# The first stage and the weight folds put into the written list, and a table that names each tile's buffer

## The chip, the cores and the metric

The kernel runs on one core of one Trainium2 chip, whose granted TensorE clock is 0.997 of full speed in the profiled execution. The metric is the device time of one execution in microseconds (us). The time before is the median of three runs, 713.57 us (712.26 to 713.77).

## The reference

A residual network of four blocks, A, B, A, B, over 2048 tokens of width 576, all in float32, each block on the layer norm of its input:

```python
x = x + A(layernorm(x))   # linear attention: 32 heads of 18; q, k, v = x @ wqkv; phi = elu + 1
x = x + B(layernorm(x))   # 32 heads; per head the best of 8 keys k1 and the best of 8 keys k2
                          # pick one of 64 experts; out = sum gelu(x . u[e]) * v[e]
x = x + A(layernorm(x))   # same weights again
x = x + B(layernorm(x))
```

In B the scores are `(x @ w_q) . k`. Since `w_q` (576 x 32 x 256) meets only the 8 keys of each half, the kernel first folds the keys into the weights: 64 products of 128 x 576 by the keys, one for each head and half. The result is a table of 576 x 448 that serves both B blocks.

## The kernel before, in words

The tokens lie in 16 tiles of 128 rows. The four blocks form two layers (l = 0 and 1), each with a front (`fT` transposes the normalised tile into a high and a low part, `k`, `v` and `q` multiply it by the projections, `st` adds phi(k) times v to the running state `kva`) and a back (`num`, `oT`, `O` for the attention output, `bT`, `S` for the transposed tile and its scores, `sel` and `gel` for the choice of experts, `po` for the output). A product of a tile with a 576-wide weight is 28 matmuls: 14 passes over high and low parts, two column ranges each (lines 269 and 504). Products are named `ppk_t`, `ppv_t`, `ppq_t`, `ppo_t` and `pps_t` after what they make and the tile.

Some transposes do not go through TensorE (the table SQUARES names them, from tile 4 on in the first front): VectorE turns 32 x 32 squares (`rf`, line 239), one DMA writes the tile to DRAM (`y_df`), and four DMAs read it back transposed (`gf`, line 248); ScalarE and VectorE then split it into `thi` and `tlo` (lines 124 and 126).

**The folds.** Group m of the 64 loads `wq_t[:, m, :]` (288 KB, 128 x 576) by one DMA (`fold_load`, line 654) and multiplies it by a 128 x 32 piece of the padded keys `kpad` (`fold_mm`, line 664). The 32 result rows of group m land in partitions `32*j` to `32*j + 32` of one PSUM tile, with j = m mod 4:

```python
        a, j = divmod(i, 4)                      # i = m % 16
            nc.tensor.matmul(p[32 * j:32 * j + 32, at:at + c1 - c0], kpad[:, ch // 2, 24 - 8 * a:56 - 8 * a],
                             st[:, c0:c1], start=(a == 0), stop=(a == 3))
```

So a fold matmul uses 32 of the array's 128 columns: column tile j. Each group has two matmuls, one of 320 columns and one of 256. Sixteen groups fill one PSUM tile; `fold_out` (line 668 on) then copies it out, transposes it and splits it into `shi` and `slo`, the score weights.

**What sets the order.** Each engine executes its instructions in the order in which the program holds them. Up to tile 10 of layer 0 a Python loop writes them: per tile t = 2 to 9 it emits the loads of eight fold groups, the products k, v and q of the tile, and then the eight fold groups m = 8(t-2) to 8(t-2)+7 in ascending order (`for m in groups: fold_mm(m)`). From there on the order is written out as a long list of pieces, `play("...")`: the word `k0.10` runs the next piece of front_k of layer 0 and tile 10, up to the point at which the piece hands back control. The pieces of PE, ScalarE, VectorE and GpSimd are tied to the order of the program in both parts (`in_order`); the DMA-issuing queue SP is tied in the list alone, and the order of the transfers of the loop is left to the framework. All transfers are issued by SP, each of which waits for the one eight before it.

**Buffers.** Each kind of tile has a ring of a few buffers (`x1` 6, `pq` 2, `x2` 2, `s` 2, `thi` and `tlo` 4 and so on), and a new tile takes the next one of its ring. The fold loads go through `x1`, `pq`, `x2` and `s`, in a fixed sequence of ten.

Of the kernel before, what the change touches and what calls it, by code (L numbers as in the profile page):

```python
# [11 lines left out]
F32 = mybir.dt.float32  # L12
# [9 lines left out]
S, D, H, DH = 2048, 576, 32, 18  # L22
# [40 lines left out]

@with_exitstack
def network(ctx, tc, x_in, wqkv, wo, wq_t, k_t, u_t, v2, c_mask, c_mask4, c_ident, c_code, c_code1, c_scale, c_shift, out):
# [5 lines left out]
    dr = ctx.enter_context(tc.tile_pool(name="dr", bufs=1, space=DRAM))  # L71

# [60 lines left out]
    BUFS = {"pq": 2, "s": 2, "x1": 6, "x2": 2}  # L133
# [514 lines left out]

    fold_ps = {}
    fold_st = {}  # L650

    def fold_load(m):
        st = fold_st[m] = stage(f"fold{m}")
        nc.sync.dma_start(st, wq_t[:, m, :])

    def fold_mm(m):
        st = fold_st.pop(m)
        ch, i = divmod(m, 16)
        if i == 0:
            fold_ps[ch] = psum(f"fold_ps{ch}")  # L660
        p = fold_ps[ch]
        a, j = divmod(i, 4)
        for c0, c1, at in ((0, 320, 0), (320, D, 512)):
            nc.tensor.matmul(p[32 * j:32 * j + 32, at:at + c1 - c0], kpad[:, ch // 2, 24 - 8 * a:56 - 8 * a],  # L664
                             st[:, c0:c1], start=(a == 0), stop=(a == 3))
# [46 lines left out]
    def small_loads():  # L712
# [16 lines left out]

    vu = {}  # L730

    def load_vu(l, t):
        sv = stage("vst")
# [3 lines left out]
        su = stage("ust")[:, :NB * NE].rearrange("p (b e) -> p b e", b=NB)  # L737
# [28 lines left out]
    def ok(t):  # L766
        return 0 <= t < NT
# [27 lines left out]
    def pair(t):  # L795
        return ((st, t - 1), (st, t)) if t % 2 else ()

    def play(text, at=0):

        for w in text.split():  # L800
# [5 lines left out]
                  fo=fold_out, bc=bc, bT=exp_y, cT=exp_c, S=S, sel=sel, gel=gel, po=po, keep=keep, rl=rl, lq=lq, ldx=ldx, ldq=ldq, base=base)  # L806
# [10 lines left out]
    with in_order(*ALL):  # L817
# [36 lines left out]
        small_loads()  # L854
        split_weight(wq_in, 0, whi, wlo, REM, (0,))
# [7 lines left out]
        PER, FIRST = 8, 10  # L863
        for t in range(2, FIRST):
            m0 = PER * (t - 2)
            groups = range(m0, m0 + PER)
            done = (m0 - 1) // 16 if m0 % 16 == 0 and m0 else None
            if t == 2:
                first_load(0, 4)
                run(0, (ln, 3))  # L870
            else:
                run(0, (fT, t + 1, 1))
            for m in groups[:4]:
                fold_load(m)
# [12 lines left out]
            run(0, (v, t), (q, t), (fT, t + 1), *pair(t))
            for m in groups:
                fold_mm(m)
    with in_order(*ALL, ET.SP):  # L890

        play("""
            lv0.0 fl0.13 fo0.3 fT0.11x2 wl1.0 ln0.12 fl0.14 fT0.11 fl0.15 ln0.12x2 ln0.13x2 lv0.0 ld0.1 v0.10 k0.10
            fT0.12x2 v0.10x2 ln0.13 k0.10x2 fo0.3 fT0.13 fT0.11 q0.10x2 fT0.11 v0.11 ln0.15 k0.11 v0.11 ld0.1 v0.11
            q0.10 q0.11 ln0.15 sv0.0 fT0.12 ln0.14x3 fT0.12 fT0.13 k0.11 ld0.0 fT0.12 k0.12 v0.12 k0.12 k0.11 st0.11
            st0.10 q0.12 k0.12 fT0.13x2 v0.12x2 ln0.15 fT0.13 fT0.15 k0.13 wl0.0 q0.12x2 k0.13x2 wl0.0 q0.10 fT0.15x3
            v0.13 fT0.15 k0.15 fT0.14 v0.15 v0.13x2 st0.12 st0.13 q0.11x2 fT0.14x3 v0.15x2 fT0.14 k0.14x2 v0.14 q0.13
            v0.14x2 k0.14 k0.15x2 st0.14 st0.15 wl0.0 ld0.2 ld0.0 wl0.0 mk0.0x2 q0.13x2 zs0.0x2 wl0.0 q0.11 num0.0x3
            M0.1x2 M0.2x2 num0.1 M0.3x2 q0.14x2 num0.0x2 oT0.0 M0.0 M0.4 num0.1 ld0.2 ld0.3x2 num0.1x3 oT0.1 oT0.0x2
            M0.0 num0.2 M0.4 oT0.0 oT0.1 O0.0 num0.2x4 O0.0x2 q0.14 oT0.2x2 O0.0x3 oT0.1x2 O0.1x3 bT0.0 num0.3 oT0.2x2  # L900
            O0.2 num0.3x3 bT0.0x2 O0.1x2 q0.12 num0.3 S0.0x2 ld0.4x2 O0.2 O0.1 bT0.1 num0.4 S0.0 num0.4x2 O0.2 bT0.1
            gel0.0x2 ld0.6 gel0.0 sel0.0 q0.15 sel0.0x2 ld0.5 q0.15 gel0.0 bT0.1 q0.15 O0.2x2 sel0.0 oT0.3x3 S0.1x3
            num0.4 cT0.0x3 num0.4 oT0.3 O0.3 O0.2 gel0.1 sel0.1x2 gel0.1x3 O0.3 bT0.2x2 po0.0x4 ld0.6 po0.0 bT0.2
            O0.3x2 sel0.1x2 oT0.4x3 S0.2x2 O0.3 S0.2 gel0.2 O0.3 oT0.4 cT0.1x2 O0.4 sel0.2 po0.0x2 fT1.0x2 cT0.1 ld0.5
            po0.1 O0.4 num0.5 po0.1 fT1.0 bT0.3x3 po0.1x2 gel0.2x2 O0.4 po0.1 O0.4 ld0.7x2 O0.4x2 q0.13 v1.0 sel0.2
            keep1.0 k1.0 v1.0x2 sel0.2 num0.5 gel0.2 sel0.2 po0.1 q0.14 po0.1 cT0.2 num0.5 cT0.2x2 fT1.1x2 k1.0
            keep1.0 S0.3x2 po0.2 num0.6 num0.5 num0.6 S0.3 gel0.3 bT0.4x2 num0.6 fT1.1 keep1.1 num0.5 keep1.1 num0.6
            po0.2x2 sel0.3 k1.0 oT0.5x2 k1.1 oT0.5x2 v1.1 num0.6 oT0.6x2 num0.7 bT0.4 po0.2 gel0.3 po0.2 sel0.3x2 S0.4
            gel0.3 S0.4 num0.7x3 gel0.3 sel0.3 v1.1 k1.1x2 v1.1 po0.2 S0.4 cT0.3x2 po0.2 gel0.4 sel0.4x2 num0.7
            gel0.4x2 cT0.3 oT0.6 ld0.8x2 oT0.6 O0.5x2 fT1.2x2 po0.3x2 fT1.2 O0.5 keep1.2 O0.5x3 bT0.5 st1.0 st1.1  # L910
            oT0.6 bT0.5 v1.2 po0.3 oT0.7 po0.3 oT0.7 bT0.5 po0.3x3 fT1.3x3 oT0.6 v1.2 num0.8x2 ld0.10 v1.2 O0.6 gel0.4
            O0.6x3 bT0.5 sel0.4x2 k1.2 bT0.5 k1.2 num0.8x2 k1.2 cT0.4x3 S0.5 fT1.3 S0.5 fT1.3 po0.4x2 O0.6x2 bT0.6
            S0.5 oT0.7 po0.4x3 gel0.5 sel0.5 bT0.6 num0.8 oT0.8x2 po0.4 oT0.7 po0.4 bT0.6 oT0.7 fT1.4x2 sel0.5 oT0.7
            v1.3 ld0.10 gel0.5x2 ld0.9 v1.3 fT1.4 v1.3 sel0.5 O0.7x2 k1.3 gel0.5 sel0.5 cT0.5 bT0.6 cT0.5 O0.7x2 st1.2
            k1.3 bT0.6 O0.7x2 cT0.5 po0.5x2 ld0.9 k1.3 fT1.4 keep1.3 bT0.7 num0.10 S0.6x3 num0.10 keep1.3 gel0.6x2
            fT1.4 v1.4 gel0.6 sel0.6x3 bT0.7 po0.5x4 oT0.8 po0.5 fT1.5 num0.10 oT0.8 num0.9x2 v1.4 gel0.6 oT0.8
            num0.10 num0.9 k1.4x2 bT0.7x2 keep1.2 num0.9x2 oT0.9 fT1.5 oT0.8 O0.8x2 bT0.7 S0.7x2 k1.4 O0.8 sel0.6
            cT0.6 O0.8 fT1.5 st1.3 fT1.5 oT0.9 cT0.6 ld0.11x2 cT0.6 po0.6 fT1.5 keep1.5 k1.5 po0.6 O0.8 oT0.9 S0.7
            gel0.7 sel0.7 O0.8 po0.6x3 bT0.8x2 sel0.7 po0.6x2 fT1.6x2 bT0.8 keep1.5 oT0.9x2 v1.5 v1.4 gel0.7 num0.10
            oT0.10x2 k1.5 sel0.7 gel0.7 k1.5 fT1.6 keep1.4 oT0.9 ld0.12 gel0.7 O0.9 sel0.7 cT0.7 st1.4 bT0.8 num0.11x2  # L920
            bT0.8 O0.9 cT0.7 O0.9x2 S0.8x2 v1.5 fT1.6 cT0.7 po0.7 fT1.6 oT0.10 keep1.6 O0.9x2 po0.7 num0.11 bT0.9
            po0.7 k1.6 po0.7x2 v1.5 po0.7 num0.11 S0.8 sel0.8 po0.7 fT1.7 oT0.10 gel0.8 bT0.9 gel0.8x2 oT0.10 num0.11
            sel0.8 ld0.12 oT0.10 fT1.7 sel0.8 k1.6 oT0.11 v1.6 bT0.9 gel0.8 sel0.8 v1.6x2 fT1.7 num0.12 k1.6 O0.10x2
            oT0.11 bT0.9x2 O0.10 keep1.4 num0.12 ld0.13 cT0.8x3 num0.12x3 O0.10x2 oT0.12 S0.9 st1.5 S0.9 fT1.7x2 po0.8
            S0.9 gel0.9 oT0.11 q0.15 po0.8 oT0.12 O0.10 bT0.10 po0.8 gel0.9 oT0.11 gel0.9 bT0.10 po0.8x3 v1.7x3
            oT0.11x2 O0.11 ld0.13 po0.8 k1.7 bT0.10x2 gel0.9 sel0.9x2 num0.13 fT1.8x3 sel0.9x2 cT0.9 st1.6 oT0.12
            O0.11x4 num0.13x2 bT0.10 num0.13 S0.10x2 num0.13 cT0.9x2 po0.9 fT1.8x2 v1.8 po0.9x3 O0.11 S0.10 gel0.10
            bT0.11x2 ld0.14x2 po0.9x2 sel0.10x2 k1.7x2 gel0.10x2 po0.9 bT0.11 oT0.13 fT1.9x2 sel0.10 k1.8 oT0.12x2
            oT0.13 bT0.11 keep1.7 bT0.11 fT1.9 oT0.12 O0.12 S0.11 k1.8 O0.12 num0.14 S0.11 gel0.10 keep1.6 sel0.10
            O0.12 v1.8x2 cT0.10 num0.14 O0.12 k1.8 ld0.15 cT0.10x2 st1.7 po0.10 oT0.13 po0.10x2 fT1.9x2 v1.9 S0.11  # L930
# [92 lines left out]
```

## Time and profile before

| What | us |
|---|---|
| median of 3 runs | 713.57 |
| the profiled execution | 712.88 |
| span of its instructions | 711.1 |
| TensorE matmuls busy | 695.5 |
| TensorE weight loads busy | 649.1 |
| VectorE busy | 466.2 |
| ScalarE busy | 321.3 |
| GpSimd busy | 202.2 |

The engines are named PE (matmuls), PEld (weight loads, which overlap matmuls), DVE (VectorE), ACT (ScalarE), POOL (GpSimd) and SP (the queue that issues DMAs). L269 is line 269 of the kernel. Matmul ends are modelled, so a record lasts longer than the matmul holds the array. In a view by time stretches, each row gives an engine's busy time in the stretch and, after the x, how many of its instructions overlap the stretch. A row of waits gives the total, the number and the longest wait in us. A row in order of time gives start, length, what ran, its shape, its count and, in brackets, the idle time before it and what ended it.

### The profile page before, as it was taken

What the parts mean: (1) busy time and instruction counts of PE and PEld (TensorE: products, weight loads), DVE (VectorE), ACT (ScalarE), POOL (GpSimd) and SP (SyncE); (2) the same over time, 40 slices, a digit from 0 to 9 for tenths busy, and PEclk for the clock granted to TensorE, in tenths of its full rate; (3) what the DMA queues carried; (4) which work ended last, traced back from release to release, by engine and by line L of the source; (5) the groups of instructions that cost most, each with busy time, mean ns of one, the idle gap of its engine ahead of it and who ended that gap; (6) DMA issues with size and microseconds to landing.
All of it is one profiled execution on the core that took longest, in us unless ns stands there. A gap on an engine that the chain in (4) does not pass through costs nothing.

```text
span 711.1 us, 14610 instructions
## 1 busy us (share of the span) xinstructions
PE 695.5 (98%) x5464; PEld 649.1 (91%) x5464; DVE 466.2 (66%) x1005; ACT 321.3 (45%) x658; POOL 202.2 (28%) x544
## 2 busy tenths in 40 slices
PE   8999999999999999999999899999999999999996
PEld 5999989998998999999999899999999999999984
DVE  5543343445327787788888687651556798888896
ACT  4522332242314455556555555543544534454443
POOL 2210100011003444434344343210144343444331
PEclk9999999999999999999999999999999999999998
DMA  9947878754230325467775666342631144311111
GB/s 268 297 136 244 278 227 258 248 158 131 93 116 18 101 72 188 126 190 221 241 232 164 213 211 185 112 142 83 205 123 53 55 124 127 103 65 51 50 69 50
DMA packets 82712, 107.17 MB, mean 151 GB/s; under 512 B 8977, under 2 KB 47377, under 8 KB 82641
## 3 DMA queue, kind: packets, MB, share of 16 engines
q1 hardware_dynamic: 82640, 106.24, 47.2%
q8 instruction: 43, 0.70, 0.4%
q14 instruction: 29, 0.23, 0.1%
HBM read 68.88 MB, written 37.32 MB: 149 GB/s over the span
## 4 chain that ended last, share of the span: by engine, by line
PE 81%; DVE 7%; DMA 4%; issue 2%; ACT 2%; SPq 1%; POOL 1%; DVEq 0%; ACTq 0%; POOLq 0%
PE ppo L504 15%; PE ppq L269 15%; PE ppk L269 13%; PE ppv L269 13%; PE pps L546 8%; PE kva L546 4%; PE kva L376 3%; PE fold_ps L664 2%; PE po L631 2%; PE ptb L225 2%; DMA y_df<-rf 2%; PE pto L225 1%; PE m L431 1%; PE ppq L281 1%; DMA xf<-in_x 1%
## 5 line engine op out<-in xcount | busy, mean ns | idle before, releaser
L504 PE MATMUL ppo<-ohi,thio 126*128 126x252 f32 (+1 forms) x320 | 50.5, 300 | 0.1
L269 PE MATMUL ppk<-whi,thif 128*128 128x252 f32 (+1 forms) x300 | 45.5, 298 | 1.4 <-ACT thif L124 1.4
L504 PEld LDWEIGHTS ppo<-ohi,thio 126*128 126x128 f32 (+1 forms) x320 | 44.8, 189 | 0.8 <-issue 0.3
L269 PEld LDWEIGHTS ppk<-whi,thif 128*128 128x128 f32 x300 | 40.9, 188 | 4.6 <-issue 2.9
L269 PE MATMUL ppv<-whi,thif 128*128 128x252 f32 (+1 forms) x300 | 44.6, 295 | 0.2 <-ACT thif L124 0.2
L269 PE MATMUL ppv<-whi,tlof 128*128 128x252 f32 (+1 forms) x300 | 44.0, 293 | 0.1
L187 POOL TENSOR_SCALAR rsf<-mvf 128x1 f32<-128x1 f32 x16 | 3.4, 213 | 142.9 <-DVE mvf L184 142.8
L269 PE MATMUL ppk<-whi,tlof 128*128 128x252 f32 (+1 forms) x300 | 43.9, 293 | 0.0
L197 ACT ACTIVATE junk<-x,mb 128x576 bf16<-128x576 f32 x32 | 24.8, 774 | 40.6 <-POOL mb L195 40.4
L269 PEld LDWEIGHTS ppv<-whi,thif 128*128 128x128 f32 x300 | 41.3, 188 | 1.4 <-ACT thif L124 0.8
L269 PEld LDWEIGHTS ppv<-whi,tlof 128*128 128x128 f32 x300 | 41.2, 188 | 0.3 <-DVE tlof L126 0.3
L269 PEld LDWEIGHTS ppk<-whi,tlof 128*128 128x128 f32 x300 | 41.2, 188 | 0.0
L471 POOL TENSOR_TENSOR o<-pq,zb 128x576 f32<-128x576 f32 x19 | 27.4, 1442 | 47.1 <-ACT zb L416 45.7
L215 ACT ACTIVATE yb<-x,rsb 128x640 f32<-128x640 f32 x32 | 29.4, 918 | 24.5 <-POOL rsb L204 24.4
L504 PE MATMUL ppo<-olo,thio 126*128 126x252 f32 (+1 forms) x256 | 39.6, 293 | 0.0
L504 PE MATMUL ppo<-ohi,tloo 126*128 126x252 f32 (+1 forms) x256 | 39.5, 293 | 0.0
L269 PE MATMUL ppq<-whi 128*128 128x252 f32 (+1 forms) x260 | 39.4, 298 | 0.0
L289 DVE TENSOR_SCALAR ek<-ek 128x576 f32<-128x576 f32 x16 | 7.3, 459 | 48.5 <-ACT ek L287 48.5
L269 PEld LDWEIGHTS ppq<-whi 128*128 128x128 f32 x260 | 36.1, 188 | 0.3
L504 PEld LDWEIGHTS ppo<-olo,thio 126*128 126x128 f32 x256 | 36.2, 189 | 0.0
L269 PE MATMUL ppk<-wlo,thif 128*128 128x252 f32 x240 | 36.1, 293 | 0.0
L269 PE MATMUL ppv<-wlo,thif 128*128 128x252 f32 x240 | 36.1, 293 | 0.0
(211 smaller groups left out, 1770.8 us busy)
## 6 DMA issues: line engine op xcount, KB each, us to landing
fold<-in_wq_t SPq DMA_DIRECT2D x64, 288.0 KB, 4.2
whi<-hl_d SPq DMA_DIRECT2D x26, 320.0 KB, 4.0
y_df<-rf SPq DMA_DIRECT2D x23, 320.0 KB, 2.3
gf<-y_df SPq DMA_DIRECT2D x92, 80.0 KB, 2.4
pq_d<-eq SPq DMA_DIRECT2D x19, 288.0 KB, 5.4
pq<-pq_d SPq DMA_DIRECT2D x19, 288.0 KB, 5.7
xf<-in_x SPq DMA_DIRECT2D x16, 288.0 KB, 4.5
x<-in_x SPq DMA_DIRECT2D x16, 288.0 KB, 3.5
```

What stands on the lines that cost most here:

```text
L197: nc.scalar.activation(junk, xt, AF.Square, bias=m[:, 0:1], accum_out=m[:, 1:2])
L215: nc.scalar.activation(y, x2, AF.Identity, scale=rs[:, 0:1], bias=rs[:, 1:2])
L225: nc.tensor.transpose(pt[:, b * P:(b + 1) * P], x, ident)
L269: nc.tensor.matmul(o[:, at:at + c1 - c0], tt[a == "lo"][:, b, :], wb[:, cols + c0:cols + c1], start=(i == 0), stop=(i == len(todo) - 1))
L281: nc.tensor.matmul(p[:, at:at + c1 - c0], tt[a == "lo"][:, b, :], wb[:, cols + c0:cols + c1], start=(i == 0), stop=(i == len(todo) - 1))
L289: nc.vector.tensor_scalar(e, e, 1.0, EPS, op0=ALU.min, op1=ALU.add)
L376: nc.tensor.matmul(a[64 * h:64 * h + 64, c * 72:c * 72 + n], vt[:, 2 * c + h], fk[:, f0:f0 + n], start=(t == 0 and c == 0), stop=(t == NT ...
L471: nc.gpsimd.tensor_tensor(o[:, :D], pq, zb, op=ALU.mult)
L504: nc.tensor.matmul(p[:, at:at + c1 - c0], hl[a][:r, b], w[:r, c0:c1], start=(i == 0), stop=(i == len(todo) - 1))
L546: nc.tensor.matmul(p[:, :512], hl[a == "lo"][:, b, :], shi[:, b] if w == "hi" else slo[:, blocks(REM)[b][1]], start=(i == 0), stop=(i == l ...
L631: nc.tensor.matmul(p[:, at:at + c1 - c0], c[i], vmix[:, c0:c1], start=(i == 0 and not based), stop=(i == 1))
L664: nc.tensor.matmul(p[32 * j:32 * j + 32, at:at + c1 - c0], kpad[:, ch // 2, 24 - 8 * a:56 - 8 * a], st[:, c0:c1], start=(a == 0), stop=(a ...
```

## The change

Three things are done together.

1. The loop over tiles 2 to 9 is gone. The pieces of these tiles stand in the written list, which is tied for SP too, and the whole list, layer 1 included, is a new one. Fold loads and fold matmuls are pieces of it (`ml0.13`, `mm0.13` for group 13). The first ten fold loads stand ahead of the list, with the loads of x tiles 4 and 5, and the four mask loads move between them.
2. The fold loads go through a sequence of 14 buffers, which takes in the two buffers of kind `o`.
3. A table SLOTS has for each kind of tile a string of digits; the n-th tile of the kind takes the buffer that the n-th digit names.

The work of each engine is the same: as many instructions of each kind on PE, DVE, ACT, POOL and SP.

```diff
+SLOTS = {
+    "x": "012012102102102012010210120102102100212010101021",
+    "x1": "012345012345021352314250312354315402145052314052310523102310214350214350124",
...
+    "thi": "0123012301320130012012031203123120101210210201212031203123012301230230230231021302",
+    "tlo": "0123012301320130012012031203213212020021010010020003330030201212010101010120310231",
...
+class Slots:
+    def __init__(self, pool, bufs):
+        self.pool, self.bufs, self.at = pool, bufs, {k: iter(v) for k, v in SLOTS.items()}
+
+    def tile(self, shape, dtype, tag, name, bufs=None):
+        bufs = bufs or self.bufs
+        if tag in self.at:
+            tag, bufs = f"{tag}_{next(self.at[tag])}", 1
+        return self.pool.tile(shape, dtype, tag=tag, name=name, bufs=bufs)
...
+    FOLD = ["x1", "pq", "x2", "s", "x1", "o", "x1", "pq", "x2", "s", "x1", "x1", "o", "x1"]
...
-    def fold_load(m):
-        st = fold_st[m] = stage(f"fold{m}")
+    def fold_load(l, m):
+        tag = FOLD[m % len(FOLD)]
+        st = wk.tile([P, D + 56 * (tag == "o")], F32, tag=tag, name=f"fold{m}", bufs=BUFS[tag])[:, :D]
+        fold_st[m] = st
         nc.sync.dma_start(st, wq_t[:, m, :])
 
-    def fold_mm(m):
+    def fold_mm(l, m):
...
-    with in_order(*ALL):
+    with in_order(*ALL, ET.SP):
...
         small_loads()
+        run(0, (fl, 4), *((fold_load, m) for m in range(6)), (fl, 5))
+        mask_loads()
+        run(0, *((fold_load, m) for m in range(6, 10)))
...
-        PER, FIRST = 8, 10
-        for t in range(2, FIRST):
-            m0 = PER * (t - 2)
-            groups = range(m0, m0 + PER)
...
-            run(0, (v, t), (q, t), (fT, t + 1), *pair(t))
-            for m in groups:
-                fold_mm(m)
-    with in_order(*ALL, ET.SP):
 
         play("""
-            lv0.0 fl0.13 fo0.3 fT0.11x2 wl1.0 ln0.12 fl0.14 fT0.11 fl0.15 ln0.12x2 ln0.13x2 lv0.0 ld0.1 v0.10 k0.10
...
+            ml0.13 ln0.4x3 ml0.18 k0.2 fl0.7 k0.2 ln0.3 fl0.9 fT0.4 ml0.11 ln0.3 k0.2 ln0.3 ml0.26 ln0.5x3 fT0.5 fT0.4
+            v0.2x2 fT0.3 q0.2 fT0.5 ln0.7x2 mm0.0 mm0.2 mm0.1 v0.2 fT0.3 mm0.6 mm0.5 fl0.6 mm0.3 fT0.3 q0.2x2 ln0.9
+            mm0.4 ln0.6 ln0.7 mm0.8 ln0.9 mm0.9 fT0.7 ml0.27 mm0.13 ml0.16 mm0.7 ml0.10 mm0.11 v0.3x3 fl0.10 k0.3 q0.3
...
```

**The folds on PE.** Before, the first eight fold groups stand on PE behind the products of tile 2. In the rows, `fold1_562` is the load of group 1, and 32x320 is a result of 32 rows and 320 columns.

```order
L664 MATMUL fold_ps0_698<-fold0_560,kpad_76 32x320
L664 MATMUL fold_ps0_698<-fold0_560,kpad_76 32x256
L664 MATMUL fold_ps0_698<-fold1_562,kpad_76 32x320
L664 MATMUL fold_ps0_698<-fold1_562,kpad_76 32x256
L664 MATMUL fold_ps0_698<-fold2_564,kpad_76 32x320
L664 MATMUL fold_ps0_698<-fold2_564,kpad_76 32x256
L664 MATMUL fold_ps0_698<-fold3_566,kpad_76 32x320
L664 MATMUL fold_ps0_698<-fold3_566,kpad_76 32x256
```

All eight runs of the loop are of this kind: the groups go through column tiles 0, 1, 2, 3 and again 0, 1, 2, 3. In the changed program PE has nine runs of 12, 4, 8, 8, 6, 10, 7, 6 and 3 groups. This is the third, behind the product k of tile 4:

```order
L712 MATMUL fold_ps1_1059<-fold16_784,kpad_76 32x320
L712 MATMUL fold_ps1_1059<-fold16_784,kpad_76 32x256
L712 MATMUL fold_ps1_1059<-fold20_952,kpad_76 32x320
L712 MATMUL fold_ps1_1059<-fold20_952,kpad_76 32x256
L712 MATMUL fold_ps1_1059<-fold18_584,kpad_76 32x320
L712 MATMUL fold_ps1_1059<-fold18_584,kpad_76 32x256
L712 MATMUL fold_ps1_1059<-fold22_963,kpad_76 32x320
L712 MATMUL fold_ps1_1059<-fold22_963,kpad_76 32x256
L712 MATMUL fold_ps1_1059<-fold26_638,kpad_76 32x320
L712 MATMUL fold_ps1_1059<-fold26_638,kpad_76 32x256
```

It goes on with groups 17, 21 and 25. Its groups follow one another by column tile: 0, 0, 2, 2, 2, 1, 1, 1. The nine runs hold these groups, in this order: (0 2 1 6 5 3 4 8 9 13 7 11), (15 10 12 14), (16 20 18 22 26 17 21 25), (19 23 29 24 27 31 30 28), (32 34 33 35 39 43), (36 47 37 41 40 44 45 38 42 46), (48 52 56 51 49 53 57), (50 54 58 62 55 60), (61 59 63).

**The turned tile 12 on SP.** Before, the write of tile 12's turned squares stands behind the loads of u (`ust`, line 740 on) for the experts:

```order
L700 DMA xf_15_1985<-in_x 128x576
L740 DMA ust_2002<-in_u_t 128x64 x2
L742 DMA ust_2002<-in_u_t 64x64
L743 DMA ust_2002<-in_u_t 64x64
L740 DMA ust_2002<-in_u_t 128x64 x2
L453 DMA x0_1_2009<-in_x 128x576
L242 DMA y_df0_12_2071<-rf0_12_2069 128x640
```

Now it stands among the fold loads, 44 rows ahead of the loads of u:

```order
L702 DMA fold51_1688<-in_wq_t 128x576
L702 DMA fold57_1690<-in_wq_t 128x576
L293 DMA gf0_9_1693<-y_df0_9_1110 32x4x160 x4
L287 DMA y_df0_12_1753<-rf0_12_1585 128x640
L748 DMA xf_13_1755<-in_x 128x576
L702 DMA fold48_1791<-in_wq_t 128x576
```

**The kept low part of tile 6 on SP.** For layer 1 some transposed tiles are written to DRAM (`front_keep`, `hl_d`), and the buffers of `thi` and `tlo` come free when the write has landed. Before, that of the low part of tile 6 stands behind the reads `gf1_9`, which wait for the write `y_df1_9`:

```order
L248 DMA gb0_11_5307<-y_db0_11_5272 32x4x160 x4
L242 DMA y_df1_9_5316<-rf1_9_5314 128x640
L242 DMA y_do0_13_5357<-ro0_13_5312 128x640
L347 DMA hl_d7_97<-thif1_7_4982 128x640
L248 DMA gf1_9_5364<-y_df1_9_5316 32x4x160 x4
L349 DMA hl_d6_96<-tlof1_6_4726 128x640
```

Now it stands 16 rows ahead of tile 11's own write `y_db0_11`:

```order
L293 DMA gb0_9_4853<-y_db0_9_4788 32x4x160 x4
L287 DMA y_df1_7_4909<-rf1_7_4858 128x640
L392 DMA hl_d6_96<-thif1_6_4731 128x640
L394 DMA hl_d6_96<-tlof1_6_4732 128x640
L293 DMA gf1_7_4927<-y_df1_7_4909 32x4x160 x4
```

More of the change, by code (lines that the diff above doesn't have):

```diff
@@ L728, in small_loads, with mask_loads @@
         nc.gpsimd.memset(digit, 63)
+    def mask_loads():
+        nc.sync.dma_start(mask[:63, :72], c_mask[:63, 7:79])
+        nc.sync.dma_start(mask[64:127, :72], c_mask[63:, 61:])
+        for r in (0, 64):
+            nc.sync.dma_start(mask[r:r + 36, 72:], c_mask[:36, 7:43])
     vu = {}
     def load_vu(l, t):
-        sv = stage("vst")
+        sv = stage("vst", 9)
         nc.sync.dma_start(sv[:64], v2)
@@ L736, in load_vu @@
         yield 1
[L737 removed]
+        su = stage("ust", 10)[:, :NB * NE].rearrange("p (b e) -> p b e", b=NB)
         for b, (r, bl) in enumerate(blocks(REM)):
```

243 lines of the change are left out of this document (129 added, 114 removed).

## The prediction

> **What bounds the kernel now.** I read the page first, then TensorE by stretches, then who it waits for.
>
> ```profile
> span 711.1 us, 14610 instructions
> PE 695.5 (98%) x5464; PEld 649.1 (91%) x5464; DVE 466.2 (66%) x1005; ACT 321.3 (45%) x658; POOL 202.2 (28%) x544
> ...
> 0.00:40.00 40.00, 36.28 (x273) 31.33 (x274) 22.92 (x39) 18.00 (x32) 9.97 (x28) 1.00 0.84 266
> 40.00:150.00 110.00, 110.00 (x1083) 100.31 (x1082) 44.36 (x89) 34.62 (x84) 8.04 (x24) 1.00 0.72 229
> 150.00:232.00 82.00, 79.67 (x671) 76.56 (x670) 39.81 (x80) 27.79 (x59) 10.36 (x23) 1.00 0.34 100
> 232.00:460.00 228.00, 226.07 (x1705) 213.41 (x1704) 178.72 (x392) 126.52 (x265) 93.97 (x247) 1.00 0.55 174
> 460.00:660.00 200.00, 199.69 (x1483) 189.94 (x1482) 139.82 (x304) 93.24 (x181) 64.71 (x174) 1.00 0.33 102
> 660.00:711.10 51.10, 43.80 (x260) 37.51 (x258) 40.59 (x105) 21.16 (x44) 15.14 (x49) 0.96 0.16 59
> ...
> PE kva L546 <- DVE tlob L126: 1.9, 1, 1.9
> ```
>
> PE is the bound: 15.6 of 711.1 us idle. The start (3.7 idle) is the same code in both programs, and its first products stand in the same order; the end (7.3 idle) is the last tiles' chain, which the new list leaves nearly as it was. Between 40 and 660 us only 4.6 us of idle time are to be had, and three waits are most of it: the 1.9 of the last row, and 1.35 and 0.63 that are quoted below. The stretch that the change rewrites, 40 to 150, has none: 110.00 of 110.00 us busy, at full clock, with the DMA engines at 0.72. So a new order can gain little there, and whatever makes PE's own work longer there is paid in full.
>
> **The change part by part.**
>
> *The folds.* Fold groups are the one work whose length on PE depends on the order. These rows are the second run of eight groups (which ends where the next product starts), then the first run, cut into short stretches:
>
> ```profile
> 62.01 2.19 PE L664 MATMUL fold_ps<-fold,kpad 128*32 128x320 f32 x32
> 64.12 0.38 PE L269 MATMUL ppk<-whi,thif 128*128 128x252 f32 x1
> ...
> L664 PE MATMUL fold_ps<-fold,kpad x256: 378/406/458, 47.4 to 149.0; 128*32 128x320 f32 x64, 128*32 128x256 f32 x64
> ...
> 47.40:47.46 0.06, 0.05 (x4) 0.05 (x6) 0.00 (x0) 1.00 0.50 115
> 47.46:47.70 0.24, 0.24 (x4) 0.13 (x8) 0.00 (x0) 1.00 0.88 326
> 47.70:47.76 0.06, 0.06 (x8) 0.05 (x4) 0.00 (x0) 1.00 0.77 307
> 48.19:48.24 0.05, 0.05 (x8) 0.04 (x1) 0.00 (x0) 1.00 0.14 46
> 48.24:48.40 0.16, 0.16 (x8) 0.07 (x1) 0.00 (x0) 1.00 0.12 43
> 48.40:48.46 0.06, 0.06 (x8) 0.05 (x6) 0.00 (x0) 1.00 0.00 0
> 49.16:49.23 0.07, 0.07 (x9) 0.00 (x0) 0.00 (x0) 1.00 0.00 0
> ```
>
> A run of eight takes 64.12 - 62.01 = 2.11 us. A group leaves 256 / 64 = 4 matmul records. In the cut rows four records begin at once (x4 at 47.40), nothing begins until 47.70, then four more (x8: four ending, four beginning), and so on; 48.19 begins the fourth round, 48.40 the first of the second four groups. So the four column tiles run side by side, and within its tile a group holds 48.40 - 47.40 = 1.00 us for its four records, one after the other; the second four begin their last record at 49.16 and are through after one more record of 0.21 to 0.22 (the distance from 48.19 to 48.40), 0.98 us after their start. I call 0.98 us a slot. A run of two slots takes 2.11 = 2 x 0.98 + 0.15 of change-over. Two groups in one tile never overlap.
>
> The row 48.24:48.40 tells how far PE looks ahead. All four tiles began their last record by 48.24, yet until 48.40 only one weight load runs, that of group 4; the other groups' loads begin at 48.40 together with the first matmul of group 4. So a group is not let in until the one before it in the program has begun. From that I take the rule of my forecast: groups begin in program order, each as soon as its tile is free and its predecessor has begun.
>
> Is a group quicker when it has the array alone? The state fold is float32 over the whole array with nothing beside it:
>
> ```profile
> 216.84 3.15 PE L431 MATMUL m<-wob,kvb 127*126 127x288 f32 x12
> 219.61 1.17 PE L269 MATMUL ppq<-whi,thif 128*128 128x252 f32 x6
> ```
>
> (219.61 - 216.84) / 12 = 0.23 us per record of 288 columns, 0.80 ns per column. A fold record takes 1.00 / 4 = 0.25 for 288 columns on the mean (320 and 256), 0.87 ns per column, with three others beside it. So the rate looks like that of a float32 record anywhere, and a lone group should still take its slot.
>
> Now the new runs. In (16 20 18 22 26 17 21 25) the tiles are 0 0 2 2 2 1 1 1. By the rule they begin in slots 0, 1, 1, 2, 3, 3, 4, 5 and the run ends after 6: 6 x 0.98 + 0.15 = 6.0 us where the loop's order took 2.11. Counted alike, the nine runs take 5, 2, 6, 4, 3, 5, 5, 4 and 2 slots, together 36: 36 x 0.98 + 9 x 0.15 = 36.6 us. Before, 8 x 2.11 = 16.9. Term: **+19.7 us**, with no idle time in the stretch to take it.
>
> The Trainium skill, "TensorE: Matmul & The Clock Gate", Part 3 on packing small matmuls, says that matmuls start and end strictly in program order. By that rule group 0's four records would end before group 1's first, a group would cost 0.98 us in any order, 64 x 0.98 = 62.7 us before and after, and the order would change nothing. This case's trace disagrees: four groups begin within 0.06 us.
>
> *State updates.* PE has 22 runs of state matmuls instead of 20, two pairs being cut in half.
>
> ```profile
> 293.84 1.43 PE L376 MATMUL kva<-ek,v 128*64 128x72 f32 x40
> 321.34 0.81 PE L376 MATMUL kva<-ek,v 128*64 128x72 f32 x20
> ```
>
> 2 x 0.81 - 1.43 = 0.19 each: **+0.4**.
>
> *The three waits.*
>
> ```profile
> 152.78 0.84 DVE L239 STREAM_TRANSPOSE rf<-yf 128x640 f32<-128x640 f32 x1 [1.34 <-ACT yf L215]
> 154.75 0.85 SPq L740 DMA_DIRECT2D ust<-in_u_t  x2
> 158.44 0.38 SPq L242 DMA_DIRECT2D y_df<-rf  x1
> 173.70 0.79 PE L269 MATMUL ppk<-whi,thif 128*128 128x252 f32 x4 [1.35 <-ACT thif L124]
> 215.55 0.72 PE L413 MATMUL z<-zc,pick 128*128 128x288 f32 x2 [0.63 <-ACT zc L395]
> 399.00 1.75 SPq L248 DMA_DIRECT2D gf<-y_df  x4
> 400.79 0.43 SPq L349 DMA_DIRECT2D hl_d<-tlof  x1
> 403.36 0.82 DVE L126 TENSOR_TENSOR tlob<-gb,thib 128x640 fp32r<-128x640 f32 x1 [5.50 <-DMA hl_d<-tlof]
> ```
>
> Tile 12's product waited 1.35: its squares were ready at 153.6, but SP issued their write at 158.44, behind the loads of u. Now the write stands 44 rows ahead of those loads and PE comes later: **-1.35**. The sum z waited 0.63 for the copy of the state that PE had just finished; now the 28 matmuls of `ppq_13` stand between: **-0.6**. The wait of 1.9 before the second part of tile 11's scores came from `tlob`, whose buffer was held by a write to `hl_d` that SP kept behind four reads. That write moves ahead, and the table gives `tlob` another buffer, one that product `ppo_12` frees just before. It may end or leave a smaller wait, so between 0 and -1.9 I take half: **-0.9**.
>
> *Other moves.* The last fold_out now stands in the ramp of the back, beside `ppo_1` and `ppo_2`:
>
> ```profile
> L683 ACT ACTIVATE shi<-fold_pt x20: 352/418/434, 73.3 to 158.3; 128x112 fp32r<-128x112 f32 x20
> L687 DVE TENSOR_TENSOR slo<-fold_pt,shi x16: 354/360/371, 74.5 to 160.1; 128x112 fp32r<-128x112 f32 x16
> 235.62 0.76 DVE L494 SCALAR_TENSOR_TENSOR x<-ppo,x 128x576 f32<-128x576 f32 x1 [2.20 <-PE ppo L504]
> 238.28 0.75 DVE L474 TENSOR_REDUCE den<-o 128x32 f32<-128x576 f32 x1 [1.17 <-POOL o L471]
> ```
>
> It costs ACT 5 x 0.42 and DVE 5 x 0.36 = 1.8 us. DVE had 2.2 + 1.2 us of idle there, and a product covers it; without that cover up to 1.8. I take **+0.2**. The fold loads (64 DMAs on SP, with the x loads, `y_df` and `gf` queued behind them) had waits of their own for PE:
>
> ```profile
> SPq L654 <- PE fold_ps L664: 13.4, 7, 4.0
> ```
>
> A run that lasts 6 us instead of 2 frees its buffers up to 4 us later, and what stands behind on SP goes out later. But PE, the reader of those transfers, is late by the same run, so this costs nothing while the list holds a product or more between a transfer and its use; uncovered, it is the fourth case below. The first ten loads issued ahead, the masks behind six of them and the `pq_d` writes held for later have no reader before the run of folds or the back: nothing.
>
> Sum: 19.7 + 0.4 - 1.35 - 0.6 - 0.9 + 0.2 = +17.4 us on the profiled execution's 712.88 us (1.8 more than its span); the median of the runs lies 0.7 above it: 713.57 + 17.4 = **731.0 us**.
>
> **The rivals.** *Independent tiles.* If each tile took its groups from a queue of its own, deep enough, a run would last as long as its fullest tile: 4, 2, 3, 3, 3, 3, 3, 4, 2 = 27 slots, 27.8 us, a term of +10.9 and a time of 722.2. For it: four tiles do run side by side. Against it: the single weight load of 48.24:48.40. The Trainium skill, "TensorEngine Tiling", Key Properties, calls the tiles independent, with weight loads and matmuls in parallel; by that rule alone this rival would hold, and the trace agrees only as far as groups already let in.
>
> *A shared stream* (the other side). If the four tiles share one path for the moving data, a group alone runs four times as fast, any order costs 2.11 / 8 = 0.26 per group, and the folds stay at 17 us. It decides from a lone group of 0.26 instead of 0.98. Then only the gains and the state updates stand: 713.57 + 0.4 - 2.65 = 711.3, 0.3% faster. For it: the trace never shows a tile alone. Against it: the state fold's 0.80 ns per column.
>
> *Transfers behind the long runs.* Four of the nine runs last 5 or 6 slots; if SP, held by their buffers, brings a turned tile late after each and PE waits 1.9 us (the longest wait quoted), that adds 7.6: 738.6. It decides once a transfer issued behind such a run is needed less than one product after it. Against it: nothing in 40 to 150 waited before.
>
> **How the numbers follow.** Forecast 0.66, independent tiles 0.13, shared stream 0.12, late transfers 0.09. The likeliest gives 731.0, with its own range from 729.8 (the last wait gone whole, nothing from the ramp: 1.2 less) to 734.9 (no gain but z, 1.8 from the ramp: 1.35 + 0.9 + 1.6 more). The range for 8 in 10 reaches down to independent tiles with the same 1.2 less, 721.0, and up to 735. About 0.2%, 1.4 us, is what a measurement of this kernel can tell from no change. Faster than that needs the shared stream: 0.11; within it, the shared stream with its gains lost: 0.03; slower: 0.86.
>
> **What would show it.** In the changed profile PE's fold runs should sum to about 36.6 us, the run that begins with group 16 lasting 6.0 and the first (12 groups) 5.0; PE busy should rise by about 20 us and all of it before the products of tile 11. The waits at z and tile 12 should be gone, those of the start and the end as before. A run of eight in 2 to 3 us would show the rule of entry or the rate of a lone tile wrong, and the forecast with it; runs as counted but a time above 735 would show that the long runs hold transfers which PE then waits for.

## The result, and the profile after

The changed kernel takes 729.38 us (median of 4 runs, 729.10 to 729.52) where the kernel before takes 713.67 us on the same chip (712.26 to 714.35): 1.0222 times as long, 95% interval 1.0205 to 1.024. The prediction was 731.0.

The page of the changed kernel, its span and its first line of busy times:

```profile
span 727.6 us, 14617 instructions
PE 717.2 (99%) x5464; PEld 661.1 (91%) x5464; DVE 467.6 (64%) x1005; ACT 319.6 (44%) x658; POOL 204.5 (28%) x544
```

The span is 16.5 us longer. (The medians differ by 15.7; the profiled execution of the kernel before, 712.88, lies 0.8 under its median.) PE is busy 21.7 us more (695.5 to 717.2) and idle 5.2 us less (15.6 to 10.4). So both halves of the forecast are there, longer work and fewer waits. The waits of PE in the changed kernel, in us (total, number, longest):

```profile
PE warm L744 <- DVE junk L860: 1.2, 1, 1.2
PE po L676 <- DVE tlob L169: 1.1, 1, 1.1
PE pps L591 <- ACT thib L167: 0.9, 1, 0.9
PE ptf L270 <- ACT yf L260: 0.8, 1, 0.8
PE ptb L270 <- DVE cg L657: 0.6, 1, 0.6
PE ptb L270 <- ACT yb L260: 0.6, 1, 0.6
PE ptf L270 <- DVE yf L258: 0.5, 1, 0.5
PE po L676 <- ACT thib L167: 0.4, 1, 0.4
```

These are the first 10 us (`warm`, `ptf`) and the last 20 (`po`, `pps`, `ptb`). Tile 12, the sum z and tile 11's scores are not among them: between 10 and 710 us PE waits for nothing longer than 0.15 us. Two stretches of that middle, as busy times of PE, PEld, DVE, ACT and POOL:

```profile
40.00:150.00 110.00, 110.00 (x895) 92.64 (x893) 45.78 (x94) 32.94 (x78) 11.43 (x33) 1.00 0.72 227
478.00:680.00 202.00, 202.00 (x1496) 192.46 (x1496) 140.53 (x309) 93.59 (x182) 67.79 (x178) 1.00 0.30 92
```

From 40 to 150 us PE is as full as before, at full clock, but 895 matmuls overlap the stretch instead of 1083. Three of the nine fold runs in order of time, each with the row that follows it:

```profile
47.11 5.17 PE L712 MATMUL fold_ps<-fold,kpad 128*32 128x320 f32 x48
52.21 0.38 PE L314 MATMUL ppv<-whi,thif 128*128 128x252 f32 x1
...
67.24 2.14 PE L712 MATMUL fold_ps<-fold,kpad 128*32 128x320 f32 x16
69.31 1.43 PE L421 MATMUL kva<-ek,v 128*64 128x72 f32 x40
...
78.17 6.07 PE L712 MATMUL fold_ps<-fold,kpad 128*32 128x320 f32 x32
84.17 0.66 PE L724 MATMUL fold_pt<-ident,foldf 128*128 128x128 f32 x4
```

From start to the next start they last 5.10, 2.07 and 6.00 us. The third holds eight groups, as every run of the loop did in 2.11 us. All nine, beside the count of the prediction:

| run | slots | slots x 0.98 + 0.15 | measured |
|---|---|---|---|
| 1 | 5 | 5.05 | 5.10 |
| 2 | 2 | 2.11 | 2.07 |
| 3 | 6 | 6.03 | 6.00 |
| 4 | 4 | 4.07 | 4.04 |
| 5 | 3 | 3.09 | 3.07 |
| 6 | 5 | 5.05 | 5.07 |
| 7 | 5 | 5.05 | 5.01 |
| 8 | 4 | 4.07 | 4.04 |
| 9 | 2 | 2.11 | 2.07 |
| sum | 36 | 36.6 | 36.47 |

The eight runs before took 16.92 us in sum, so the folds cost 19.55 us more. That is more than the whole difference. The waits above 0.15 us give 4.9 us back. The products (k, v, q and the attention output) take 3.0 us more, measured from matmul start to matmul start without those waits: 477.85 us before, 480.81 after. What is left, 1.1 us less, lies in small groups (the transposes alone are over 1 us shorter, others longer) and was not looked into. 19.55 - 4.9 + 3.0 - 1.1 = 16.5.

The 3.0 us of the products were in no theory of the prediction. Rows of two products of the kernel before, behind one another (the first of the three rows of each, 28 matmuls in all):

```profile
186.31 1.46 PE L269 MATMUL ppk<-whi,thif 128*128 128x252 f32 x10
189.95 1.46 PE L269 MATMUL ppv<-whi,thif 128*128 128x252 f32 x10
```

And in the changed kernel, first one from 56 us, then two from 181 us:

```profile
56.03 1.50 PE L314 MATMUL ppk<-whi,thif 128*128 128x252 f32 x10
59.77 1.50 PE L314 MATMUL ppq<-whi,thif 128*128 128x252 f32 x10
...
180.87 1.46 PE L314 MATMUL ppk<-whi,thif 128*128 128x252 f32 x10
184.51 1.49 PE L314 MATMUL ppk<-whi,thif 128*128 128x252 f32 x10
188.23 1.47 PE L314 MATMUL ppv<-whi,thif 128*128 128x252 f32 x10
```

A product lasts 3.64 us before; in the changed kernel some last 3.74 (from 56.03) or 3.72 (from 184.51) and others still 3.64 (from 180.87), with no idle time in them. The last group of experiments is about these.

### The profile page after: what moved, and what is told of

Same layout as the page of the kernel before. It is cut to its first block, busy times and chain, and to the rows that moved or that the text cites. A ratio compares the mean times of both kernels' runs of the same rounds, so it can differ in the third digit from the quotient of the medians.

```text
span 727.6 us, 14617 instructions
## 1 busy us (share of the span) xinstructions
PE 717.2 (99%) x5464; PEld 661.1 (91%) x5464; DVE 467.6 (64%) x1005; ACT 319.6 (44%) x658; POOL 204.5 (28%) x544
## 4 chain that ended last, share of the span: by engine, by line
PE 93%; DVE 3%; DMA 1%; ACT 1%; issue 1%; POOL 1%; SPq 0%; DVEq 0%; POOLq 0%
PE ppo L549 16%; PE ppv L314 15%; PE ppq L314 15%; PE ppk L314 15%; PE pps L591 8%; PE fold_ps L712 5%; PE kva L591 5%; PE kva L421 3%; PE po L676 2%; PE ptb L270 2%; PE pto L270 2%; PE m L476 1%; PE ppq L326 1%; DMA wst<-in_wqkv 1%; DMA xf<-in_x 1%
## 5 line engine op out<-in xcount | busy, mean ns | idle before, releaser
L376 ACT ACTIVATE v<-ppv 128x252 f32<-128x252 f32 x64 | 20.5, 375 | 38.4 <-PE ppv L314 37.3
L712 PE MATMUL fold_ps<-fold,kpad 128*32 128x320 f32 (+1 forms) x256 | 37.1, 409 | 0.0
L549 PEld LDWEIGHTS ppo<-ohi,tloo 126*128 126x128 f32 x256 | 36.4, 188 | 0.0
```

The source lines that it names most:

```text
L376: nc.scalar.activation(vt[:, c:c + 4, :63], x.rearrange("p (c e) -> p c e", c=4), AF.Copy)
L549: nc.tensor.matmul(p[:, at:at + c1 - c0], hl[a][:r, b], w[:r, c0:c1], start=(i == 0), stop=(i == len(todo) - 1))
```

## Experiments

Every kernel here computes the whole network. The kernel before ran beside each of them; its median lay between 712.17 and 713.06 us. A pair is two successive product matmuls, of 252 and 324 columns.

### Is it the order of the column tiles?

**The same runs, tiles in turn.** In the changed kernel a table TURN gives each label of the list another group; places, loads and buffers stay. Each run keeps its groups, but they follow one another by tiles in turn.

```diff
+    TURN = [...]
     def fold_load(l, m):
...
-        nc.sync.dma_start(st, wq_t[:, m, :])
+        nc.sync.dma_start(st, wq_t[:, TURN[m], :])
     def fold_mm(l, m):
         st = fold_st.pop(m)
+        m = TURN[m]
```

> The changed kernel, but inside each of the nine runs the groups of that run are given out so that the column tiles take turns (each place of the list loads and multiplies another group of the same run; places, buffers and all other work stay). Entry in program order (my theory): the runs shrink from 36 slots to what their fullest tile holds, 4, 2, 3, 4, 3, 3, 3, 4, 2 = 28 slots, 28 x 0.98 + 9 x 0.15 = 28.8 us against the 36.5 measured, so the time falls by 7.7 us to about 721.7. Independent tiles: they would have taken no more than their fullest tile before, so nothing changes: 729.4.

Measured: 721.08 us (720.71 to 721.89), 1.012 times before (1.0098 to 1.0142). The runs last 4.01, 2.06, 3.07, 4.00, 3.04, 3.09, 3.06, 4.00 and 2.06 us, 8.1 less than in the changed kernel; the time fell by 8.3. Had the tiles taken their groups from queues of their own, the changed kernel would have had these lengths already. Independent tiles are refuted.

**Ascending groups.** The same edit with a table that puts all 64 groups in ascending order into the places of the list.

> The changed kernel with the 64 groups given out in ascending order along the same places of the list (the first place multiplies group 0, the next group 1 and so on; places, run lengths, buffers and all other work stay). By the count the nine runs take 3, 1, 2, 2, 2, 3, 2, 2, 1 = 18 slots, 18 x 0.98 + 9 x 0.15 = 19.0 us, 17.5 less than measured. If the waits that went away at tile 12, at z and at tile 11's scores went away because of the new list and the buffer table, they stay away: 729.4 - 17.5 = 711.9, 0.2% under the kernel before. If they went away because the long runs made PE late and so gave every transfer more time, they come back (1.35 and 1.9) and new ones can appear between 40 and 180 us: 713.5 to 717.

Measured: 711.75 us (711.51 to 712.12), 0.9988 times before (0.9978 to 0.9997). The third run, in order of time:

```profile
74.94 2.18 PE L715 MATMUL fold_ps<-fold,kpad 128*32 128x320 f32 x32
77.06 0.76 PE L727 MATMUL fold_pt<-ident,foldf 128*128 128x128 f32 x5
```

2.12 us instead of 6.00 for eight groups in the same place. The whole loss is the order of the groups: 17.6 us came back, 1.9 more than the change had cost. And PE waits for nothing above 0.15 us between 9 and 693 us here either. So the list and the table ended the three waits; they were not covered by PE being late.

**Pairs and twos in the kernel before.** The loop emits its eight groups in another order, nothing else.

```diff
-            for m in groups:
-                fold_mm(m)
+            for g in (0, 4, 1, 5, 2, 6, 3, 7):
+                fold_mm(groups[g])
```

> The kernel before with one line changed: each run of eight groups is multiplied in the order 0 4 1 5 2 6 3 7, whose column tiles are 0 0 1 1 2 2 3 3. Entry in program order: starts in slots 0, 1, 1, 2, 2, 3, 3, 4, so 5 slots or 5.05 us a run instead of 2.11, 8 x 2.94 = +23.5 us: 737.2 if the waits at tile 12 and at tile 11's scores stay as they are, 734.0 if a late PE alone makes them vanish (1.35 and 1.9). Independent tiles or any look-ahead of a few groups: every tile holds two groups as before, 713.7. A shared stream: 713.7 too.

Measured: 734.80 us (734.06 to 735.98), 1.0311 times before (1.029 to 1.0332). The second run:

```profile
64.84 5.13 PE L664 MATMUL fold_ps<-fold,kpad 128*32 128x320 f32 x32
69.89 1.33 PE L269 MATMUL ppk<-whi,thif 128*128 128x252 f32 x8
```

5.05 us, and all eight runs 5.06, within a hundredth of what five slots give. The time rose by 22.4 where the runs alone add 23.5. With PE so late tile 12's wait shrank from 1.35 to 0.23 us, while one of 0.46 came before a product q of the first front; the rest of the difference was not looked into. The waits at z (0.63) and at tile 11's scores (1.74) stayed.

With the order 0, 1, 4, 5, 2, 3, 6, 7:

> The kernel before with one line changed: each run of eight groups in the order 0 1 4 5 2 3 6 7, column tiles 0 1 0 1 2 3 2 3. Entry in program order: starts in slots 0, 0, 1, 1, 1, 1, 2, 2, so 3 slots or 3.09 us a run, 8 x 0.98 = +7.8 us: 721.5, or down to 718.3 if a late PE makes the two waits vanish. If instead PE looks ahead past two groups whose tile is taken, 2 slots and 713.7.

Measured: 719.95 us (718.67 to 721.62), 1.0103 times before (1.0079 to 1.0126); all runs 3.10 us. The rule of entry holds in both kernels and for every order tried.

**Fuller runs.** Ascending groups, and four fold words moved to a neighbouring run.

```diff
-... mm0.39 mm0.43 st0.5 ... mm0.36 fT0.8x2 ... mm0.47 mm0.37
+... mm0.39 mm0.43 mm0.47 mm0.36 st0.5 ... fT0.8x2 ... mm0.37
-... mm0.57 fT0.10 ... mm0.50 ... mm0.60 fT0.14 ... mm0.61
+... mm0.57 mm0.50 fT0.10 ... fT0.14 ... mm0.60 mm0.61
```

> The changed kernel with its groups in ascending order (as in the run before with ascending order, 18 slots), and four groups moved between neighbouring runs, so that the nine runs hold 12, 4, 8, 8, 8, 8, 8, 4 and 4 groups: 3, 1, 2, 2, 2, 2, 2, 1 and 1 slots, together 16. My rule (groups enter in program order, a slot is 0.98 us): 16 x 0.98 + 9 x 0.15 = 17.0 us of folds instead of 19.0, so 711.75 - 2.0 = 709.8 us, 0.4% faster than the kernel before. Rival, buffers: two groups are used earlier (their load may not have landed) and two later (their buffers come free later); if PE then waits for a load, the gain is lost: 711.5 or more, and a wait of a fold group for its DMA shows in the list of waits.

Measured: 709.96 us (709.49 to 710.03), 0.9965 times before (0.9953 to 0.9978). The folds take 17.06 us for 16 slots, as counted.

### What ended the three waits?

**No table.** The kernel with ascending groups (711.75), with `SLOTS.clear()` ahead of the pools.

> The changed kernel with ascending groups (711.75 us), and the table of buffers emptied: each kind of tile goes round its ring again; the list stays. Theory A (the list alone ended the three waits, the table does nothing by itself): 711.8, within 0.2%. Rival B (the wait of 1.9 us before the second part of tile 11's scores was ended by the buffer that the table gives to tlob): that wait comes back, 713.6. Rival C (the table puts the tiles where the products read them more slowly: product matmuls took 3.3 us more in sum with the list and the table than before, with no wait): products fall back to 114 and 146 ns for a pair of matmuls, 708.5.

Measured: 711.33 us (710.54 to 711.60), 0.9984 times before (0.9975 to 0.9994). This looks like theory A, but two things cancel in it. First tile 11's scores, in order of time, then tile 13's:

```profile
400.11 0.82 DVE L170 TENSOR_TENSOR tlob<-gb,thib 128x640 fp32r<-128x640 f32 x1
...
401.41 1.31 PE L592 MATMUL kva<-shi,tlob 128*128 128x512 f32 x5
...
431.78 0.43 SPq L395 DMA_DIRECT2D hl_d<-tlof  x1
...
434.75 0.82 DVE L170 TENSOR_TENSOR tlob<-gb,thib 128x640 fp32r<-128x640 f32 x1 [2.35 <-DMA hl_d<-tlof]
...
435.63 0.96 PE L592 MATMUL kva<-shi,tlob 128*128 128x512 f32 x3 [1.46 <-DVE tlob L170]
```

At tile 11 there is no wait. (The nine `tlob` made from `gb` are those of tiles 5 to 13; the one at 400.11 is the seventh and the one at 434.75 the last.) So the wait that the kernel before had there stays away without the table: the list ended it, as it ended those at z and tile 12, and B as it was put is refuted. But two tiles later a wait of the same kind appears, 1.46 us, held by a write to `hl_d` out of the buffer that `tlob` takes, and two of 0.44 and 0.41 us come before products v of layer 0 and 1. So the table keeps the new list from making waits of its own, 2.3 us here. Against it the products fell from 480.9 to 477.5 us, so the table also slowed them (C).

**Three words.** The kernel before, with three moves in its list.

```diff
-... lv0.0 ld0.1 v0.10 k0.10 fT0.12x2 v0.10x2
+... v0.10 k0.10 fT0.12x2 lv0.0 ld0.1 v0.10x2
-... v0.14 q0.13 v0.14x2 ... mk0.0x2 q0.13x2 zs0.0x2
+... v0.14 v0.14x2 ... mk0.0x2 q0.13x3 zs0.0x2
-... keep1.6 O0.9x2 ... keep1.6 sel0.10
+... keep1.6x2 O0.9x2 ... sel0.10
```

> The kernel before, loop and buffers as they were, with three words moved in its list: the loads of u behind the write of tile 12's turned squares; the product q of tile 13 from ahead of v of tile 14 to ahead of the sum z; the write of tile 6's kept low part straight behind that of its high part. My theory (each of the three waits is held by one row of the list and by nothing else): -1.35 - 0.63 - 1.87 = -3.85 on 712.45, so 708.6 us, 0.5% faster than before and ahead of the changed list with ascending groups. Rival (something else is late right behind each: the squares of tile 12, which were ready only 1.3 us after PE's need, or other tiles' transfers behind the moved writes): the waits shrink but come back elsewhere, 710.5 to 712.5.

Measured: 710.92 us (709.26 to 711.98), 0.9977 times before (0.9968 to 0.9985). The three waits are gone but for 0.21 us at tile 12, which makes 3.6. Half of it came back in front of the last state updates:

```profile
208.28 0.83 PE L376 MATMUL kva<-ek,v 128*64 128x72 f32 x20 [0.47 <-ACT v L331]
210.50 0.81 PE L376 MATMUL kva<-ek,v 128*64 128x72 f32 x20 [1.39 <-DVE ek L290]
```

The product that now covers z had covered the evacuation of the last k and v. The rival had the right kind, though not its place. The write of the low part, moved in the list, ends the wait for `tlob` here with the rings as they were, which agrees with the run without the table.

### Why do the same products take longer?

The table names buffers, so it also decides where in SBUF they lie. In the changed program two of the four `thi` and two of the four `tlo` stand behind the two buffers of kind `o`, which are 2528 bytes wide per partition; the other large tiles are multiples of 256. No trace shows an address: these places are worked out from the widths of the tiles in the program, and which buffer a product reads from the digits of the table. In the traces the pace goes by the buffer: 261.2 to 261.8 ns for a pair from the buffers at multiples of 256 bytes, 265.1 to 265.5 from those 224 past one, 266.3 to 266.4 at 192 (means over all products, from start to start).

**Wider o.** The regrouped kernel with the buffers of kind `o` 2560 bytes wide.

```diff
-        o = wk.tile([P, D + 56], F32, tag="o", name="o" + n)
+        o = wk.tile([P, D + 64], F32, tag="o", name="o" + n)
...
-        st = wk.tile([P, D + 56 * (tag == "o")], F32, tag=tag, name=f"fold{m}", bufs=BUFS[tag])[:, :D]
+        st = wk.tile([P, D + 64 * (tag == "o")], F32, tag=tag, name=f"fold{m}", bufs=BUFS[tag])[:, :D]
```

> The regrouped kernel (709.96 us) with one size changed: the two buffers of kind o are 2560 bytes wide per partition instead of 2528, so that every buffer of thi and tlo, which the table had put behind them, begins at a multiple of 256 bytes (in the changed kernel two of the four pairs began 224 and 192 bytes past one). My theory: the products read their stationary tiles more slowly from those two places. In the changed kernel a pair of product matmuls (252 and 324 columns) took 261.2 to 261.8 ns from the buffers at multiples of 256, 265.1 to 265.5 at 224 and 266.3 to 266.4 at 192; with 337 and 328 pairs there, 337 x 4.0 + 328 x 5.1 = 3.0 us: 707.0 us, 0.7% faster than the kernel before. Rival: the slower matmuls come from what runs beside them, and the buffers' numbers only go along with that: 710.0, with as many slow matmuls as before (about 710 of 3500).

Measured: 705.87 us (705.65 to 706.21), 0.990 times before (0.9887 to 0.9914): the fastest kernel of this study, ahead of both. The means of all buffers of `thi` and `tlo` are now at 260.4 to 261.8 ns a pair, and the products take 477.25 us. Here the same two products from one tile:

```profile
53.22 1.46 PE L314 MATMUL ppk<-whi,thif 128*128 128x252 f32 x10
56.86 1.46 PE L314 MATMUL ppq<-whi,thif 128*128 128x252 f32 x10
```

3.64 us instead of 3.74. The gain of 4.1 is 3.5 in the products and 0.5 in the scores, which read the same buffers.

The same edit in the changed kernel itself:

> The changed kernel itself, its order and its slow fold runs as they are, with the buffers of kind o 2560 instead of 2528 bytes wide per partition, and nothing else: all stationary tiles of the products begin at multiples of 256 bytes. By the place of the stationary tile: 729.4 - 3.0 (worked out from the pairs) to - 4.1 (what the same edit brought in the regrouped kernel), so 725.3 to 726.4 us. Rival (the edit helped the regrouped kernel in another way, by its order): 729.4.

Measured: 725.48 us (725.35 to 725.95), 3.9 less than the changed kernel. In both kernels the 32 bytes are worth what the pairs say, or a little more.

**64 bytes in the kernel before.** An unused tile of 64 bytes laid ahead of `thi` and `tlo`.

```diff
+    pads = []
...
+        if not pads:
+            pads.append(wk.tile([P, 16], F32, tag="pad", name="pad", bufs=1))
         hi = wk.tile([P, nb, P], F32R, tag=tag + "hi", name=f"thi{n}", bufs=4 if tag == "t" else 1)
```

> The kernel before (712.17 us) with 64 unused bytes per partition laid ahead of the buffers of thi and tlo, so that all eight begin 64 bytes past a multiple of 256 instead of at one (so do the four buffers of the keys' phi and what lies behind them); nothing else. My theory (the place of the stationary tile sets the pace): 1570 pairs of product matmuls at 4 to 5 ns more each, +6.3 to +8.0 us: 719.3. Rival (what runs beside them): 712.2. A third possibility: 64 bytes are no worse than 0 and only 192 and 224 are, 712.2 as well, but with e8 at 707.

Measured: 719.54 us (718.22 to 721.40), 1.0099 times before (1.0082 to 1.0115). Two products:

```profile
187.16 1.49 PE L273 MATMUL ppk<-whi,thif 128*128 128x252 f32 x10
190.86 1.48 PE L273 MATMUL ppv<-whi,thif 128*128 128x252 f32 x10
```

3.70 us where the unshifted kernel took 3.64; pairs at 264.9 to 266.4 ns from all eight buffers. With the order of the program untouched, what runs beside the products can hardly be the cause.

**The weights at multiples of 256 too.** In the aligned kernel `zc`, `unit`, `mhalf` and `kraw` move behind `olo`, so that `whi`, `wlo`, `ohi` and `olo` start at 0 instead of 160 past a multiple of 256.

> The aligned kernel (705.87 us) with its constants laid in another order, so that the four weight tiles (whi, wlo, ohi, olo), which the products stream past the stationary tile, begin at multiples of 256 bytes too instead of 160 past one; some stationary tiles of layer 1 lie in whi (they are the ones of 263.7 ns a pair in every trace). If only the stationary tile's place counts: 178 pairs x 2.4 ns = 0.4 us less, 705.4, which is hardly told from 705.9, and those pairs at 261 ns. Rival (the streamed tile's place counts as much): each of 1750 pairs some 2 ns less or more, 702 or 709.

Measured: 710.13 us (709.88 to 710.26), 0.9969 times before (0.9957 to 0.9981), so 4.3 us slower than the aligned kernel. The means of all buffers went to 263.7 to 264.4 ns a pair, those at a multiple of 256 among them:

```profile
184.97 1.48 PE L314 MATMUL ppk<-whi,thif 128*128 128x252 f32 x10
...
188.65 1.48 PE L314 MATMUL ppk<-whi,thif 128*128 128x252 f32 x10
```

3.68 us. My theory that the stationary tile should lie at a multiple of 256 falls here; it had fitted three runs by chance, since the streamed weights lay at 160 in all of them. What fits all is the distance from the streamed tile to the stationary one, modulo 256:

| streamed at | stationary at | distance | ns a pair | kernel |
|---|---|---|---|---|
| 160 | 0 | 96 | 260.4 to 261.8 | before, changed (half), wider o |
| 160 | 224 | 64 | 265.1 to 265.5 | changed (a quarter) |
| 160 | 192 | 32 | 266.3 to 266.4 | changed (a quarter) |
| 160 | 160 | 0 | 263.7 | layer 1's tiles kept in `whi`, every kernel with `whi` at 160 |
| 160 | 64 | 160 | 264.9 to 266.4 | 64 bytes ahead of `thi` |
| 0 | 0 | 0 | 263.7 to 264.4 | weights moved |
| 224 | 64 | 96 | 260.4 to 261.7 | both moved (below) |

**Both moved.** The kernel before with 64 unused bytes ahead of `whi`, so that streamed and stationary tiles move together.

```diff
+    cp.tile([P, 16], F32, name="pad")
     whi = cp.tile([P, NB, 3 * D], F32R, name="whi")
```

> The kernel before with 64 unused bytes per partition laid ahead of the weight tiles, so that the stationary tiles lie 64 bytes further, just as in the run that cost 7 us, but the streamed weight tiles do too. Distance theory (what counts is how far apart the stationary and the streamed tile lie, modulo 256; so far 96 bytes: 261 ns a pair, 64: 265.3, 32: 266.3, 0: 263.8, 160: 265.8): the distance is 96 again, pairs at 261 ns, and the time that of the kernel before, 712.2. Place theory (each tile's own place counts): the stationary tiles are where they cost 265.8 ns a pair, and the streamed ones at a new place: 719.5, or more.

Measured: 713.60 us (711.93 to 714.88), 1.0013 times before (1.0004 to 1.0023). Two products:

```profile
185.63 1.46 PE L270 MATMUL ppk<-whi,thif 128*128 128x252 f32 x10
189.27 1.46 PE L270 MATMUL ppv<-whi,thif 128*128 128x252 f32 x10
```

3.64 us again, with every stationary tile where it had cost 3.70. The distance decides, not the place. Three limits belong to this. Modulo 128 fits the table as well as modulo 256: 160 would then be 32, and their paces overlap. The distance is that of the first matmul of a pair; the second streams from 1008 bytes further on. And the figures are means: at 96 some 85% of the pairs inside a product last 259 to 261 ns (wider o, both moved), but only 23% at 160 (64 bytes ahead of `thi`) and at 0 (weights moved), where the middle nine tenths spread from 261 to 273 and from 255 to 269 ns (waits left out). So the distance does not set the time of a single pair. Five distances were seen; what lies between them, and which part of PE or of the memory makes the difference, stays open.

## Why the prediction was right

**The folds (+19.7; measured +19.55).** Right, run by run. The rule of entry came from one row, the stretch 48.24:48.40, in which all tiles had begun their last record and only one weight load ran. Four orders since, in two kernels, gave the lengths that the rule counts. A lone group does keep its slot: in the run that begins with group 16 six slots hold eight groups, and it takes 6.00 us. The shared stream (0.26 us a group) is refuted by that row.

**Independent tiles.** Refuted. My count of this rival was one slot short: the fourth run has groups 19, 23, 27 and 31 in tile 3, so 28 slots and 723.2 us. It changed nothing in the forecast. The prediction's 62.7 us for strict program order is too high by that very order: group 1's first matmul could still run beside group 0's second, so a change of tile would cost less than 0.98 us and the order would count there too. The 0.26 us a group of the loop's runs is far from both.

**The three waits (-2.85; measured -4.3 with the small ones in the middle).** Tile 12 and z went as predicted. Mis-sized was the wait for `tlob`: -0.9 taken as half, -1.9 measured, whole. The moved write was enough for it: it stays away in the run without the table, and in the kernel before the move alone ended it. The table's other buffer, which the prediction named beside the move, was not needed there. Two more waits of 0.2 us, at `pto` and `ppv`, went too.

**State updates (+0.4).** Each half takes 0.74 us from start to start against 1.36 for a whole: 0.13 each by this count, +0.26 for two, not 0.4; the records I subtracted overlap their followers by 0.07. In sum the 22 runs take only 0.02 us more than the 20 before (waits above 0.15 us left out), since two of those had lasted 0.07 and 0.17 longer than their like.

**The ramp of the back (+0.2).** No wait there in the changed kernel: nothing.

**Transfers behind the long runs.** No wait between 10 and 710 us, so none of the 7.6 us.

**The start and the end, taken as unchanged.** The start has 0.9 us less idle time, the end 0.3 more. The first cannot be put down to the change: in the profile of the kernel with both tiles moved, whose start is that of the kernel before, it is 1.7 us less as well.

**What the sum did not hold: the products, +3.0.** The diff's table was read as a matter of waits alone. That it moves buffers in SBUF, and that the pace of a matmul hangs on it, was no step of the prediction. The 731.0 came out near 729.4 because this term stands against 2.0 us of idle time that went beyond the forecast and 1.1 us in small groups. That these nearly cancel is luck; the folds' +19.55 is not.

## What to carry to other kernels

Small matmuls on column tiles run side by side only as far as the next groups in the program find their tiles free; before a scheduler's order is taken, count its slots, as a run of eight groups can last 2.1 or 6.0 us without a wait showing. A table or a ring that names buffers also lays them out: after such a change compare the length of the same product before and after, and look at the distance between stationary and streamed operand, where 32 bytes in the width of an unrelated tile were worth 4 us of 710. When a wait is removed by taking cover from elsewhere, look at who stood under that cover.

## What was not expected of the hardware

The mean pace of float32r matmuls depends on where their two operands lie relative to one another: 261 ns a pair at a distance of 96 bytes modulo 256, 263.7 to 264.4 at 0, 265 to 266 at 32, 64 and 160. The Trainium skill, "SBUF — State Buffer", in Who interferes with whom, gives TensorE two independent read ports, one for the moving operand and one for weight loads, and says that PE never waits on anyone. If that holds for TensorE's own two reads, the distance could not matter; the traces disagree, by 0.04 to 0.10 us of the 3.64 us of a product, and by 6.5 us of the whole time when the products' stationary tiles, all but those in `whi`, were moved by 64 bytes.
